# A gated linear attention and a two-layer block on one core: state sums moved from TensorE to VectorE, a new written-out order, and matmuls of a constant with itself

## The chip, the cores and the metric

The kernel runs on one core of one Trainium2 chip. A core has five engines that this kernel uses: TensorE (matrix products; its result goes to PSUM, eight banks), VectorE, ScalarE (activation functions), POOL (GpSimd) and SP (SyncE, which here only issues DMAs). The profile calls them PE, DVE, ACT, POOL and SP; PEld is TensorE's loading of weights. Each engine works through its own queue in the order in which the program was written, and waits at semaphores for the others. The metric is the time of one execution on the device in microseconds (us).

## The reference

Four inputs q, k, v and f_logit, each of shape (4, 8, 768, 48): batch, heads, steps, head dimension. For every head a state of 48 x 48 is carried over the steps, and its output goes through a two-layer block:

```python
f = 1.0 / (1.0 + np.exp(-f_logit))
for t in range(S):
    state = f[:, :, t, :, None] * state + np.einsum('bhd,bhe->bhde', k[:, :, t], v[:, :, t])
    y[:, :, t] = np.einsum('bhd,bhde->bhe', q[:, :, t], state)
x = y.transpose(0, 2, 1, 3).reshape(B * S, H * D)      # 3072 x 384
h = x @ w_in                                            # 384 x 2048
g = 0.5 * (h + np.sqrt(h * h + 4.0))
out = g @ w_out                                         # 2048 x 384
```

## The kernel before

**Blocks.** The 3072 rows are worked on in 12 blocks p of 256 steps; three blocks make one batch entry, so the state starts anew at p = 0, 3, 6 and 9. A block is held as two chunks (cc = 0 and 1) of 64 pairs of steps, for all 8 heads. Block 0 is loaded and prepared in two halves of four heads (`FINE`), named x = 0 and 1.

**Preparing a block.** `lf`, `lq`, `lk`, `lv` load 384 KB each (SP's queue). `ex` takes exp(-f), `ut` adds 1 (VectorE), `tt` multiplies the two steps of a pair, `ln` takes the logarithm (ScalarE). `hi` rounds it to float16 and `lo` keeps the rest, so that `cu` (TensorE, lines 234 and 239) can form cumulative sums over the chunk from two float16 terms. Block 0 (`DIRECT`) takes float32 terms instead, without `hi` and `lo`. `ep` and `ea` are exponentials of these sums, `ge`, `gs`, `gb` the small decay factors of a chunk. `qu`, `ku`, `qm`, `km` multiply q and k by these (POOL or VectorE, all at the helper's line 138; `qm` and `km` are two instructions each), `vc` casts v.

**Attention of a block.** For blocks 0 to 3 `tp` transposes q and k on TensorE and `te` copies them out of PSUM; from block 4 on a transposing DMA (`tx`) does it. `sc` forms the scores, `pm` masks them (VectorE), `yt` multiplies them by v. `kv` forms what the chunk adds to the state. `yn` adds q times the incoming state `sn` to `yt`'s result, and `yc` copies y out. Blocks 0 to 3 transpose y on TensorE (`xp`, `xe`), the others by DMA (`xx`).

**The state.** The incoming state is added to `kv`'s sum in PSUM by a product with the identity, `ia` (TensorE, line 394). VectorE then multiplies the sum, from PSUM, by a factor: `sa` (line 401) gives the state for the second chunk, `sb` (line 408) that for the next block. `ia` is issued for every chunk but the first of a batch entry, 20 in all.

**The two layers.** For a block there are eight pieces `m1` (six products of 256 columns each, line 470) that put h into PSUM, `sq` and `rt` on ScalarE (square; square root over two pieces), `gt` on VectorE (line 495), and eight pieces `m2` (four products of 384 columns each, line 507) that add up the output of the two chunks; `ev` copies it out and `st` stores it. The weights are loaded by POOL's queue (`wi0` to `wi3`, `wo0` to `wo7`).

**The order.** The pieces above are only described in `describe`. The text `ORDER` names each in the order in which it is issued, with the engine that does it and the PSUM banks that it gets: `cu1.0:T@10` is the sum of block 1 on TensorE into banks 1 and 0. A piece that may run on several engines runs on the one named there. `TABLE:e` and `TABLE:s` load ScalarE's tables. The loop at line 608 goes through this text and issues the pieces; semaphores follow from the tiles that they read and write. The blocks overlap: while m1 and m2 of block p run, blocks p + 1 to p + 3 are prepared.

Of the kernel before, what the change touches and what calls it, by code (L numbers as in the profile page):

```python
# [18 lines left out]
DIRECT = [0]  # L19
# [3 lines left out]
NHL = 2  # L23
NQK = 3
DEPTH = {'f': 3, 'q': 3, 'k': 3, 'v': 3, 'UT': 3, 's': 2, 'ep': 2, 'ea': 2, 'v16': 4, 'ge': 3, 'gs': 4, 'gb': 3, 'qkT0': 2, 'qkT1': 2, 'pm00': 2, 'pm01': 2, 'pm10': 2, 'pm11': 2, 'sn0': 2, 'sn1': 2, 'y16': 2, 'xT': 5, 'hsq': 3, 'r16': 3, 'g': 4, 'os': 2}
# [6 lines left out]
ln2.0:A vc0.1:A lq2.0:S hi2.0:P pm0.00:D ep1.0:A gs0:P lo2.0:P ge1:A pm0.10:D vc0.0:A pm0.01:D ea1.0:A kv0:T@32 km1.0:P  # L32
ex3.0:A cu2.0:T@41 pm0.11:D lk2.0:S sa0:D yt0:T@60 ge2:A gs1:D yn0.1:T yc0.0:A qu1.0:D gb2:P lv1.0:S ep2.0:A qm1.0:D wi1:P
yc0.1:A ea2.0:A xp0.1:T@5 wi2:P xp0.0:T@7 ut3.0:D tp1.0:T@36 ex4.0:A lf5.0:S xe0.0:D tt3.0:P xe0.1:D te1.0.0:A te1.1.0:D
m1.0.0:T@4 wo3:P ln3.0:A ut4.0:D m1.0.1:T@0 wi3:P sq0.0:A qu2.0:D sc1.1:T@17 sq0.1:A hi3.0:P pm1.11:D TABLE:s rt0.0:A lo3.0:P
m1.0.2:T@5 pm1.10:D ia0.1:T lv2.0:S gb1:D cu3.0:T@3 tt4.0:D ku2.0:P sc1.0:T@67 sb0:D m1.0.3:T@1 pm1.00:D sq0.2:A pm1.01:D
sq0.3:A m1.0.4:T@2 km2.0:P rt0.1:A gt0.1:D m1.0.5:T@6 gt0.0:D sq0.5:A lk3.0:S gt0.3:D sq0.4:A vc1.0:P c13.0:D rt0.2:A gt0.2:D
qm2.0:P kv1:T@70 TABLE:e ep3.0:A gt0.5:D ia1.0:T yt1:T@41 sa1:D yn1.0:T lk4.0:S m1.0.6:T@5 gt0.4:D wo0:P ex5.0:A yn1.1:T
yc1.0:D ia1.1:T tp2.0:T@67 wo1:P lk5.0:S ea3.0:A ut5.0:D m1.0.7:T@2 vc2.0:P ln4.0:A te2.0.0:D xp1.0:T@4 ge3:A sq0.7:A sb1:D
tt5.0:P kv2:T@36 yc1.1:A te2.1.0:D sq0.6:A xp1.1:T@0 gs3:P ia2.0:T xe1.0:D gs2:P sc2.0:T@17 ln5.0:A wo2:P xe1.1:D sa2:D  # L40
TABLE:s rt0.3:A sc2.1:T@40 lq3.0:S wo4:P pm2.00:D ia2.1:T m1.1.0:T@3 ku3.0:P pm2.11:D m1.1.3:T@6 pm2.10:D m1.1.1:T@1 sq1.0:A
pm2.01:D m1.1.5:T@0 hi4.0:P sq1.1:A lv3.0:S gt0.7:D lo4.0:P yt2:T@47 rt1.0:A gt0.6:D yn2.1:T m1.1.2:T@2 hi5.0:P sq1.3:A
gt1.1:D wo5:P m2.0.00:T@5 lf6.0:S sq1.2:A yc2.1:D m2.0.10:T@1 ku5.0:P rt1.1:A gt1.0:D m1.1.7:T@7 sq1.5:A gt1.3:D m1.1.6:T@3
# [24 lines left out]
ln10.0:A m2.4.13:T ku9.0:P pm6.01:D ln11.0:A kv7:T@46 sq5.1:A ev4.1:D yt6:T@70 TABLE:s rt5.0:A ia7.0:T yc6.0:D yn6.1:T gs7:P
# [54 lines left out]
def describe(nc, W, ctx_tiles, aps):  # L123
# [4 lines left out]
    def eng(e):  # L128
        return getattr(nc, ENGINES[e])
# [23 lines left out]
    for p in range(NP):  # L153
# [9 lines left out]
        for x, (h0, h1) in enumerate(parts):  # L163
# [483 lines left out]
```

## Time and profile before

| | |
|---|---|
| time, median of 3 runs | 206.72 us (206.17 to 207.64) |
| the profiled execution: time | 205.34 us |
| the profiled execution: span from the first to the last instruction | 203.6 us |
| mean granted TensorE clock | 0.954 of full speed |
| DMA: moved | 32.87 MB, mean 161 GB/s over the span |
| costliest groups: m1 products (L470) | 576, 74.0 us |
| m2 products (L507) | 384, 71.6 us |
| VectorE `gt` (L495) | 96, 62.2 us |
| ScalarE `sq` (L479) and `rt` (L485) | 96 and 48, 54.7 and 50.6 us |
| POOL q and k products (L138, with ea and ep) | 40, 39.7 us |

The page of the profile gives the busy time of each engine, the span in 40 slices with a digit for the busy share, the chain of waits that ended last, and groups of instructions by line. A timeline row reads: start, duration, engine, line, operation, output and inputs, shape, count; in brackets the idle time before it and what ended that. A row of the chain reads: start, duration, engine, output, line, count. Matmuls are pipelined: their single durations overlap, so what one holds TensorE for is read from the distance of starts, as the chain does. A row of stretches gives the busy time and in brackets the number of instructions for each engine, then the granted clock, the DMA share and GB/s.

### The profile page before, as it was taken

How to read it: one execution, taken by the hardware profiler on the slowest of the kernel's cores; microseconds unless marked ns; L12 is line 12 of the kernel's file. 1: busy time of each engine (PE TensorE's matmuls, PEld its weight loads, DVE VectorE, ACT ScalarE, POOL GpSimd, SP SyncE). 2: the span in 40 equal slices, each digit the busy share in tenths (PEclk: the TensorE clock that was granted, in tenths of full speed). 3: DMA queues.
4: the chain of work that ended last, by engine and by line, in shares of the span. 5: the costliest groups of instructions: out<-in, count | busy, mean ns of one | idle time of the engine just before them, and what ended most of it. 6: DMA issues, size and time to landing. Idle time of an engine off the chain costs nothing.

```text
span 203.6 us, 5630 instructions
## 1 busy us (share of the span) xinstructions
PE 177.7 (87%) x2302; PEld 129.1 (63%) x2302; DVE 147.3 (72%) x285; ACT 154.9 (76%) x248; POOL 108.6 (53%) x135
## 2 busy tenths in 40 slices
PE   0556898799899999979999979789998999999990
PEld 0544575587657766757667857467775778677660
DVE  7649579999688997957978958818984778434650
ACT  4266679999958999769988987758886698968700
POOL 4226789899969979929679738695000000000001
PEclk9995579999999999999999999969999999999998
DMA  6999999999959799994899999932894100505305
GB/s 158 269 262 244 275 198 217 234 256 273 183 156 234 108 254 203 222 278 99 129 214 207 249 129 240 195 51 36 149 140 119 39 5 0 42 0 155 77 22 136
DMA packets 80537, 32.87 MB, mean 161 GB/s; under 512 B 73888, under 2 KB 80496, under 8 KB 80512
## 3 DMA queue, kind: packets, MB, share of 16 engines
q1 hardware_dynamic: 76688, 29.27, 69.1%
q0 software_dynamic: 3824, 3.24, 9.9%
q8 instruction: 18, 0.29, 0.6%
q14 instruction: 7, 0.06, 0.1%
HBM read 25.17 MB, written 4.72 MB: 147 GB/s over the span
## 4 chain that ended last, share of the span: by engine, by line
issue 32%; PE 26%; POOL 18%; DMA 15%; ACT 3%; DVE 2%; SPq 2%; POOLq 0%
PE ps L507 10%; POOL qk L138 6%; PE ps L470 6%; DMA q<-in_q_dram 4%; PE ps L234 4%; POOL k L138 4%; DMA xT<-y 3%; DMA wout<-in_moe_w_out_dram 3%; DMA v<-in_v_dram 2%; POOL wout L149 2%; DMA f<-in_f_logit_dram 2%; POOL v L135 2%; POOL hl L214 2%; PE ps L364 1%; PE ps L383 1%
## 5 line engine op out<-in xcount | busy, mean ns | idle before, releaser
L470 PE MATMUL ps<-xT,win 128*128 128x256 f16 x576 | 74.0, 277 | 5.1 <-DMA xT<-y 3.5
L495 DVE SCALAR_TENSOR_TENSOR g<-ps,r 128x512 f16<-128x512 f32 x96 | 62.2, 682 | 17.5 <-ACT r L485 17.3
L507 PE MATMUL ps<-wout,g 128*128 128x384 f16 x384 | 71.6, 326 | 2.4 <-DMA wout<-in_moe_w_out_dram 1.3
L479 ACT ACTIVATE hsq<-ps 128x512 f16<-128x512 f32 x96 | 54.7, 593 | 18.0 <-PE ps L470 17.3
L470 PEld LDWEIGHTS <-win 128*128 128x128 f16 x576 | 55.5, 99 | 17.2 <-DMA xT<-y 4.2
L485 ACT ACTIVATE r<-hsq 128x1024 f16<-128x1024 f16 x48 | 50.6, 1056 | 1.1
L507 PEld LDWEIGHTS <-g 128*128 128x128 f16 x384 | 36.2, 98 | 22.6 <-issue 1.7
L371 DVE TENSOR_TENSOR pm<-ps,mask 128x512 f16<-128x512 f32 x48 | 30.8, 682 | 5.2 <-PE ps L364 5.0
L527 POOL DMA_DIRECT2D out_dram<-os x1 | 0.6, 602 | 59.7 <-ACT os L133 59.7
L138 POOL TENSOR_TENSOR qk<-q,ea 128x384 f16<-128x384 f32 x20 | 19.9, 1014 | 4.7 <-DVE q L138 4.7
L138 POOL TENSOR_TENSOR qk<-k,ep 128x384 f16<-128x384 f32 x20 | 19.8, 1013 | 0.3 <-ACT ge L302 0.2
L138 POOL TENSOR_TENSOR k<-k,UT 128x768 f32<-128x768 f32 x10 | 18.1, 1815 | 1.7 <-DMA k<-in_k_dram 1.6
L178 ACT ACTIVATE f<-f 128x768 f32<-128x768 f32 (+1 forms) x13 | 10.3, 795 | 3.3 <-DMA f<-in_f_logit_dram 3.2
L138 POOL TENSOR_TENSOR UT<-UT 128x384 f32<-128x384 f32 (+1 forms) x8 | 7.8, 984 | 8.9 <-DVE UT L185 8.9
L214 POOL TENSOR_TENSOR hl<-s,hl 128x384 f16<-128x384 f32 x11 | 10.0, 912 | 4.8 <-ACT hl L133 4.7
L133 ACT COPY os<-ps 128x384 f32<-128x384 f32 x12 | 5.8, 480 | 8.6 <-PE ps L507 7.2
L401 DVE TENSOR_TENSOR sn<-ps,gs 128x384 f16<-128x384 f32 x12 | 6.6, 554 | 7.7 <-PE ps L383 5.3
L135 POOL CAST v<-v 128x768 f16<-128x768 f32 x10 | 8.2, 821 | 5.2 <-DMA v<-in_v_dram 5.2
L364 PE MATMUL ps<-qkT 48*64 48x128 f16 x384 | 9.4, 228 | 0.7 <-ACT qkT L133 0.6
L135 DVE COPY os<-ps 128x384 f32<-128x384 f32 x12 | 6.5, 552 | 4.8 <-PE ps L507 3.1
L262 ACT ACTIVATE ep<-ps 128x384 f32<-128x384 f32 (+1 forms) x13 | 6.0, 470 | 5.2 <-PE ps L239 5.0
L364 PEld LDWEIGHTS <-qkT 48*64 48x64 f16 x384 | 6.4, 110 | 4.9 <-issue 3.5
(74 smaller groups left out, 200.8 us busy)
## 6 DMA issues: line engine op xcount, KB each, us to landing
f<-in_f_logit_dram SPq DMA_DIRECT2D x11, 384.0 KB, 6.2
k<-in_k_dram SPq DMA_DIRECT2D x11, 384.0 KB, 5.4
q<-in_q_dram SPq DMA_DIRECT2D x11, 384.0 KB, 6.2
v<-in_v_dram SPq DMA_DIRECT2D x11, 384.0 KB, 5.2
out_dram<-os SPq DMA_DIRECT2D x22, 192.0 KB, 3.5
win<-in_moe_w_in_dram POOLq DMA_DIRECT2D x4, 384.0 KB, 7.5
wout<-in_moe_w_out_dram POOLq DMA_DIRECT2D x8, 192.0 KB, 6.5
f<-in_f_logit_dram SPq DMA_DIRECT2D x2, 192.0 KB, 2.9
```

Of the source, the lines that this page charges most:

```text
L135: eng(e).tensor_copy(out=o, in_=i)
L138: eng(e).tensor_tensor(out=o, in0=a, in1=b, op=ALU.mult)
L178: nc.scalar.activation(out=t, in_=t, func=AF.Exp, scale=-1.0)
L214: eng(e).tensor_tensor(out=hl[:, 1, hs, 0:D], in0=T["s", p][:, hs], in1=hl[:, 0, hs, 0:D], op=ALU.subtract)
L234: nc.tensor.matmul(out=o, lhsT=tri[:, m], rhs=t[:, hs, 0:D], start=(r == 0), stop=(r == len(terms) - 1))
L364: nc.tensor.matmul(out=T["sc", p, i, h][64 * cc:64 * cc + 64, j, :], lhsT=t[r, 1, j, i, :], rhs=t[r, 0, j], start=True, stop=True)
L371: nc.vector.tensor_tensor(out=T["pm", p, i, h], in0=T["sc", p, i, h], in1=K["mask"][:, i].unsqueeze(1).broadcast_to([128, 4, 128]), op=ALU ...
L470: nc.tensor.matmul(out=T["h", p, m][:, a], lhsT=K["win"][m // 2][:, j, m % 2 * 256 + a * 128:m % 2 * 256 + a * 128 + 128], rhs=T["xT", p][ ...
L479: nc.scalar.activation(out=T["hsq", p, r][:, a], in_=T["h", p, m].rearrange("p a c t -> p (a c t)"), func=AF.Square, scale=1.0)
L485: nc.scalar.activation(out=T["r16", p, r], in_=T["hsq", p, r], func=AF.Sqrt, scale=0.25, bias=1.0)
L495: nc.vector.scalar_tensor_tensor(out=T["g", p][:, 2 * m:2 * m + 2, :].rearrange("p a t -> p (a t)"), in0=T["h", p, m].rearrange("p a c t - ...
L507: nc.tensor.matmul(out=T["o", p, cc], lhsT=T["g", p][:, jn, cc * 128:(cc + 1) * 128], rhs=K["wout"][jn // 2][:, jn % 2, :], start=(jn == 0 ...
```

## The change

Four things change.

- **State sums.** For blocks 3 to 11 (`SADD`) `ia` is no longer issued: 15 fewer products, 5 are left. A new piece `sp` on VectorE adds the incoming state to `kv`'s sum, from PSUM into an SBUF tile `st`; it is issued 12 times, where the sum is needed further on. `sa` or `sb` then multiplies `st` by the factor, on POOL in all 12 cases. The first chunk of a batch entry needs no sum; there, and in blocks 0 to 2, `sa` and `sb` stay on VectorE and read PSUM.
- **Block 0** is no longer in `DIRECT`: its cumulative sums come from float16 terms as in the other blocks. `hi` is written by ScalarE as a second logarithm, straight into float16 (`HI_ACT`); `lo` is added. The float32 copies of the constants are no longer made, and the triangles come from four VectorE instructions instead of eight (`tri2` is laid out with its two parts exchanged).
- **A new order.** `ORDER` is written anew: another order on every queue, SP's and POOL's too, other banks, and another engine for 75 of the pieces that both orders have, `sa` and `sb` among them. Net of all moves VectorE gives up 5 `gb` and `gs`, 3 `tt`, 3 `qu`, 1 `qm` and gets 3 `ku`, 5 `lo` (one of them a new one of block 0), 1 `km`; the weight loads are issued as wi0, wi2, wi1, wi3 and wo4, wo0, wo1, wo2, wo5, wo3, wo6, wo7. In block 0 `ex1` stands behind the four logarithms. Of the last block's four stores the two of the first chunk go to POOL's queue and the two of the second to SP's; before, one of the second went to POOL's and the others to SP's.
- **Constant matmuls.** A word `wmN:T@b` in the order issues N products of the float16 identity (128 x 128) with itself into bank b; nothing reads them. There are five such words: 27 ahead of block 0's transposes, 4 ahead of `cu1`, 26 ahead of `kv0` (bank 3), 4 ahead of `xp0.0`, 5 ahead of the first `m1`. That makes 66.

Pieces for lists that are empty here (`SPLIT`, `PMACT`) are left out of the diff below.

```diff
-DIRECT = [0]
+DIRECT = []
+SADD = [3, 4, 5, 6, 7, 8, 9, 10, 11]
+HI_ACT = [0]
...
-lf0.1:S lf0.0:S lf1.0:S lk0.0:S lk0.1:S TABLE:e ex0.1:A lq0.1:S ut0.1:D ex0.0:A tt0.1:D lq0.0:S ut0.0:D lf2.0:S tt0.0:P
-ex1.0:A lv0.1:S ku0.0:D ln0.0:A lv0.0:S ln0.1:A cu0.0:T@01 ut1.0:D cu0.1:T@01 ku0.1:D ep0.0:A qu0.1:P lk1.0:S ea0.0:A tt1.0:D
-ea0.1:A qu0.0:D ge0:A ep0.1:A qm0.0:D lf3.0:S ln1.0:A km0.0:D ex2.0:A km0.1:D tp0.0:T@23 hi1.0:A lq1.0:S qm0.1:D te0.1.0:A
-lo1.0:P tp0.1:T@23 te0.0.0:A te0.1.1:D lf4.0:S wi0:P te0.0.1:A ut2.0:D sc0.0:T@45 tt2.0:D sc0.1:T@67 cu1.0:T@10 ku1.0:D
...
+lf0.0:S lf0.1:S lk0.1:S lf1.0:S lk0.0:S TABLE:e ex0.0:A lq0.0:S ut0.0:D ex0.1:A tt0.0:P lq0.1:S ut0.1:D hi0.0:A lv0.0:S
+tt0.1:D ln0.0:A hi0.1:A lo0.0:D lf2.0:S ln0.1:A ku0.1:D cu0.0:T@01 ex1.0:A lo0.1:P ku0.0:D cu0.1:T@01 ep0.0:A lk1.0:S km0.0:D
+qu0.0:P ut1.0:D ea0.1:A lq1.0:S ep0.1:A tt1.0:D qu0.1:D ln1.0:A qm0.1:D lv0.1:S ea0.0:A km0.1:D ex2.0:A qm0.0:D wm27:T@2
+tp0.1:T@23 hi1.0:A lf3.0:S ut2.0:D tp0.0:T@23 ge0:A te0.1.1:A lo1.0:D tt2.0:P te0.1.0:A te0.0.1:D wm4:T@4 cu1.0:T@45 lf4.0:S
+te0.0.0:A ku1.0:D lk2.0:S wi0:P ln2.0:A sc0.1:T@67 sc0.0:T@10 ge1:A vc0.0:A gs0:P pm0.10:D qu1.0:P hi2.0:A lq2.0:S pm0.01:D
+vc0.1:A wi2:P lo2.0:D ea1.0:A wm26:T@3 kv0:T@32 pm0.11:D ex3.0:A cu2.0:T@60 qm1.0:P pm0.00:D ep1.0:A ea2.0:A sa0:D lv1.0:S
+yt0:T@57 km1.0:D yn0.1:T gb1:P yc0.0:A yc0.1:A wm4:T@4 xp0.0:T@4 ut3.0:D wi1:P ep2.0:A xp0.1:T@1 tp1.0:T@03 ge2:A xe0.1:D
+ex4.0:A tt3.0:P xe0.0:D te1.0.0:D wm5:T@5 m1.0.1:T@5 gs2:P ln3.0:A ut4.0:D m1.0.0:T@7 sq0.1:A hi3.0:P te1.1.0:D ia0.1:T
+m1.0.4:T@6 sq0.0:A lf5.0:S gs1:P gb2:P sb0:D TABLE:s rt0.0:A sc1.0:T@14 ku2.0:P sc1.1:T@03 pm1.01:D m1.0.5:T@2 pm1.10:D wi3:P
+km2.0:D sq0.5:A m1.0.2:T@4 tt4.0:P lq3.0:S sq0.4:A gt0.0:D m1.0.3:T@0 rt0.2:A pm1.11:D lo3.0:P lv2.0:S pm1.00:D sq0.2:A
+vc1.0:P cu3.0:T@7 gt0.4:D sq0.3:A rt0.1:A qu2.0:P gt0.5:D kv1:T@31 ia1.0:T c13.0:D yt1:T@62 qm2.0:P TABLE:e ep3.0:A sa1:D
+yn1.0:T gt0.3:D ia1.1:T yn1.1:T lk3.0:S m1.0.6:T@3 yc1.0:D ex5.0:A wo4:P gt0.2:D tp2.0:T@06 ge3:A wo0:P lq4.0:S ut5.0:D
...
+m2.10.13:T m2.11.03:T ev10.1:D m2.10.03:T ev11.0:D m2.11.11:T st11.0.1:P ev10.0:A m2.11.12:T st10.01.1:S st11.0.0:P
+st10.01.0:S m2.11.13:T ev11.1:A st11.1.1:S st11.1.0:S
...
+                    direct = p in HI_ACT
+
+                    def hi(e, bk, x=x, hs=hs, p=p, direct=direct):
+                        o = K["hl"][p % NHL][:, 0, hs, 0:D]
+                        if direct:
+                            nc.scalar.activation(out=o, in_=T["UT", p][:, 1, hs], func=AF.Ln)
+                        else:
+                            copy(e, o, T["s", p][:, hs])
...
-                                         stop=(i == 1 and j == 3 and first and cc == 0), skip_group_check=True)
+                                         stop=(i == 1 and j == 3 and (p in SADD or (first and cc == 0))), skip_group_check=True)
...
+            added = p in SADD
+            if not (cc == 0 and first) and not added:
                 def ia(e, bk, cc=cc, p=p):
...
+            if added and not (cc == 0 and first):
+                def sp(e, bk, cc=cc, p=p):
+                    T["st", p, cc] = sb(f"st{cc}", p, [128, 4, 2, 48], FP32)
+                    nc.vector.tensor_tensor(out=T["st", p, cc], in0=T["u", p, cc], in1=T["sn", p, cc], op=ALU.add)
...
+                def sm(e, bk, cc=cc, p=p, nxt=nxt, factor=factor):
+                    T["sn", nxt[0], nxt[1]] = sb(f"sn{1 - cc}", nxt[0], [128, 4, 2, 48], FP16)
+                    mul(e, T["sn", nxt[0], nxt[1]], T["st", p, cc], factor())
...
-        for x in range(2):
-            nc.vector.tensor_scalar(out=tri[l, x, m], in0=tri2[l, 1 - x], scalar1=1.0, scalar2=None, op0=ALU.subtract)
-            nc.vector.tensor_copy(out=tri[g, x, m], in_=tri2[g, 1 - x])
...
+        nc.vector.tensor_scalar(out=tri[l, :, m], in0=tri2[l], scalar1=1.0, scalar2=None, op0=ALU.subtract)
+        nc.vector.tensor_copy(out=tri[g, :, m], in_=tri2[g])
...
+            if name.startswith("wm"):
+                t = ps(banks, [128, 128], FP32)
+                for n in range(int(name[2:])):
+                    nc.tensor.matmul(out=t, lhsT=ident, rhs=ident, start=True, stop=True)
+                continue
             W.pieces[name].emit(e or W.pieces[name].eng, banks)
```

More of the change, by code (lines that the diff above doesn't have):

```diff
@@ L389, in describe @@
         for cc in range(2):
-            if cc == 0 and first:
-                pass
-            else:
+            added = p in SADD
+            if not (cc == 0 and first) and not added:
                 def ia(e, bk, cc=cc, p=p):
@@ L603, in ps @@
         return psp.tile(shape, dt, name=f"ps{bank}", tag=f"ps{bank}", bufs=1)
-    K = {"s32": s32, "tri32": tri32, "ind32": ind32, "hl": hl, "qk": qk, "tri": tri, "ind": ind, "half": half, "ident": ident, "mask": mask, "win": win, "wout": wout}
+    K = {"s32": s32, "l32": l32, "tri32": tri32, "ind32": ind32, "hl": hl, "qk": qk, "tri": tri, "ind": ind, "half": half, "ident": ident, "mask": mask, "win": win, "wout": wout}
     W = Work()
```

436 lines of the change are left out of this document (242 added, 194 removed).

## The prediction

> **What bounds the kernel now.** I read the page first (busy shares and slices), then the stretches by ten microseconds, then the chain of waits, and last the timeline of the places where TensorE stands still. The profiled execution took 205.34 us, 203.6 of them its span; the median of the three runs shown is 206.72, so 1.38 is added to whatever the sum gives for the profiled execution.
>
> ```profile
> PE 177.7 (87%) x2302; PEld 129.1 (63%) x2302; DVE 147.3 (72%) x285; ACT 154.9 (76%) x248; POOL 108.6 (53%) x135
> ...
> PEclk9995579999999999999999999969999999999998
> ```
> ```profile
> 0.00:10.00 10.00, 2.54 (x8) 2.55 (x9) 6.78 (x33) 3.67 (x6) 3.71 (x14) 1.00 0.94 213
> 10.00:20.00 10.00, 6.19 (x90) 4.29 (x90) 6.84 (x16) 6.21 (x17) 4.03 (x6) 0.72 1.27 253
> 20.00:30.00 10.00, 8.89 (x138) 6.40 (x136) 6.41 (x14) 6.95 (x13) 7.99 (x11) 0.60 1.13 241
> 30.00:40.00 10.00, 7.96 (x165) 5.98 (x163) 9.63 (x18) 9.74 (x16) 9.02 (x10) 1.00 1.15 220
> 40.00:50.00 10.00, 9.83 (x148) 7.68 (x142) 9.15 (x18) 9.79 (x15) 9.88 (x14) 1.00 1.24 262
> 50.00:60.00 10.00, 8.69 (x117) 5.85 (x115) 7.71 (x16) 7.69 (x14) 7.82 (x8) 1.00 0.78 164
> ...
> 57.70:199.00 141.30, 135.88 (x1687) 97.70 (x1684) 102.63 (x178) 110.90 (x172) 66.85 (x77) 0.99 0.68 136
> ```
>
> Columns: stretch, length, then busy time of PE, PEld, DVE, ACT and POOL (instructions in brackets), granted clock, DMA share, GB/s. Three stages can be seen. Up to 30 us nothing is full but the DMA engines: the first block goes from engine to engine, and TensorE runs half its time at a reduced clock. From 30 to 50 VectorE, ScalarE and POOL are all above 90%. From 57.7 to the last matmul TensorE is busy 135.88 of 141.30 us: there it is the bound, and what leaves TensorE's queue there leaves the time. It stands still for 5.42 us in that stage, nearly all of it in four places:
>
> ```profile
> 88.04 0.83 PE L470 MATMUL ps<-xT,win 128*128 128x256 f16 x6 [1.47 <-DMA xT<-y]
> ...
> 120.97 0.82 PE L507 MATMUL ps<-wout,g 128*128 128x384 f16 x4 [1.13 <-DVE g L495]
> ...
> 133.21 0.93 PE L470 MATMUL ps<-xT,win 128*128 128x256 f16 x6 [2.00 <-DMA xT<-y]
> ...
> 157.53 0.52 PE L383 MATMUL ps<-v,qk 64*128 64x96 f16 x16 [0.76 <-ACT os L133]
> ```
>
> **The change part by part.**
>
> *State sums.* For blocks 3 to 11 the 15 products `ia` with the identity go. In the chain such a product holds TensorE between these two lengths:
>
> ```profile
> 77.62 0.27 PE ps L394
> ...
> 101.21 0.16 PE ps L394
> ```
> ```profile
> L401 DVE TENSOR_TENSOR sn<-ps,gs 128x384 f16<-128x384 f32 x12 | 6.6, 554 | 7.7 <-PE ps L383 5.3 <-PE ps L394 2.3
> ...
> L408 DVE TENSOR_TENSOR sn<-ps,gb 128x384 f16<-128x384 f32 x8 | 4.4, 550 | 0.5 <-PE ps L394 0.5
> ...
> L138 POOL TENSOR_TENSOR q<-q,UT 128x384 f32<-128x384 f32 x6 | 6.0, 997 | 0.0
> ```
>
> 15 x 0.16 to 15 x 0.27 is 2.4 to 4.0; the middle, 15 x 0.21 = 3.15, is my value. All 15 lie after 57 us, in the stage that TensorE bounds. VectorE keeps its number of state instructions: 20 multiplications before; after, 8 multiplications and 12 new sums `sp`, of the same size and one PSUM input, so 12 x 0.55 = 6.6 us goes and 6.6 comes. The 12 other multiplications go to POOL. The trace has none there on a state tile; the nearest row, a POOL product of 128x384, is 0.997 us, so POOL gains 12.0 us. After 57.7 it is busy 66.85 of 141.30, so these cost nothing while the waits between the engines have slack (the slower rival is where they have none). `sa` and `sb` read `sp`; `yn` of the second half waits for `sa`, and behind `yn` on TensorE's queue stand the m1 and m2 products.
>
> *Block 0.* Its cumulative sums were float32 products; now they are float16 products of a high and a low part:
>
> ```profile
> 7.46 2.93 PE ps L234 x8
> 10.38 1.12 PE ps L239 x8
> ...
> 69.59 0.33 PE ps L234 x2
> 69.91 0.18 PE ps L239 x8
> ```
> ```profile
> 8.61 0.93 POOL L138 TENSOR_TENSOR q<-q,UT 128x192 f32<-128x192 f32 x1 [2.08 <-DMA q<-in_q_dram]
> ...
> 12.11 0.36 DVE L138 TENSOR_TENSOR qk<-q,ea 128x192 f16<-128x192 f32 x1 [2.35 <-ACT ea L262]
> ```
>
> The float32 products took 2.93 + 1.12 = 4.05 us. The float16 ones are eight of half the width of the row at 69.59 (8 x 0.083 = 0.66) and sixteen of the narrow kind (16 x 0.0225 = 0.36): 1.02. The path gets 3.0 shorter on TensorE and longer by `lo`, a product of 128x192 like the 0.36 row, and a second logarithm about as long: 0.7. ScalarE's `ex1` is also moved behind these logarithms, and VectorE's constants lose their float32 copies. But the q products cannot go ahead of q's load: the first of them ran at 12.11 and could run no earlier than 8.61 + 0.93 = 9.54. Bounds of the gain 0 to 2.6; I take 2.0, near the upper end, since the sum of the parts (3.0 - 0.7) is 2.3.
>
> *The constant matmuls.* The order holds 27 + 4 + 26 + 4 + 5 = 66 of them, one more than the title says.
>
> ```profile
> 14.30:28.00 13.70, 10.71 (x172) 7.49 (x171) 9.95 (x20) 8.73 (x19) 10.01 (x14) 0.50 1.19 252
> ...
> 134.00:135.00 1.00, 1.00 (x6) 0.65 (x5) 0.00 (x0) 0.82 (x2) 1.00 (x2) 0.50 0.05 8
> ```
> ```profile
> L340 PEld LDWEIGHTS <-qk x4: 92/94/95, 12.5 to 12.5; 64*128 64x128 f16 x4
> ```
> ```profile
> L340 PEld LDWEIGHTS <-qk x14: 102/126/128, 14.7 to 15.0; 64*128 64x128 f16 x14
> ```
> ```profile
> 24.38 0.82 PE L454 MATMUL ps<-ident,y 128*128 128x128 f16 x6 [0.90 <-ACT y L133]
> ```
> ```profile
> 69.42 0.17 PE ps L454 x3
> ```
>
> From 14.3 to 28.0 the granted clock is 0.50, and TensorE's 10.71 busy us would be 5.4 at full clock. Not all of the difference is on the path: in the same stretch VectorE has 9.95 us of work and POOL 10.01, so the stretch of 13.7 cannot get shorter than about 10. Bounds 0 to 3.7; I take the middle, 2.0. What the 66 cost: a product of this shape takes 0.17 / 3 = 57 ns at full clock and at most 0.82 / 6 = 137 ns at half, so 3.8 to 9.0 us in all, in time when TensorE waits (3.8 of its 10 us from 10 to 20). 27 stand ahead of block 0's transposes, which wait for VectorE. The 26 are the ones to watch: they write bank 3, so they wait for the copies of the transposes out of it, and `kv0` and all of TensorE's queue stand behind them for 1.5 us (26 x 57 ns), or 3.6 if the clock is at half. `kv0` waits for ScalarE's two `vc0` anyway; at full clock I cost them at nothing.
>
> [...]
>
> *The new order.* [...] I take 1.0 gained, with bounds from 5 gained to 5 lost. From 30 to 50 us the three full engines have the same work as before, with the DMA engines at 220 to 262 GB/s: of the 4.0 gained at the start I count 1.0 given back there, for loads that then have to come earlier.
>
> *The end.* Both last stores go to SP's queue, where before POOL took one:
>
> ```profile
> 198.80 1.25 SPq L527 DMA_DIRECT2D out_dram<-os  x2
> 198.97 0.48 ACT L133 COPY os<-ps 128x384 f32<-128x384 f32 x1 [5.77 <-PE ps L507]
> 199.74 0.60 POOL L527 DMA_DIRECT2D out_dram<-os  x1 [59.66 <-ACT os L133]
> ```
>
> SP's last issue ended at 200.05; a second one of 1.25 / 2 = 0.6 ends at 200.65, POOL's ended at 200.34: 0.3 lost.
>
> *Sum.* 3.15 + (2.0 + 2.0 - 1.0) + 1.0 - 0.3 = 6.85 us. The span becomes 196.75, the profiled execution 198.5, the median 206.72 - 6.85 = 199.9.
>
> **The rivals.** (1) *Only the 15 products count.* The start is hidden by the loads and by the full stage, and the clock falls anyway in another window: 206.7 - 3.15 + 0.3 = 203.9, give or take 1.5. For it: DMA share above 1.1 from 10 to 50. Against: TensorE is the longest wait there, not a load. (2) *All of it comes.* Start 2.6 + 3.7, products 3.15, gaps 3: 206.7 - 12.45 + 0.3, about 194.5; with part of it, 196 to 198. (3) *Slower: the state path on POOL.* POOL takes its queue in order, and a pair of its q or k products is 2 x 0.997 = 2.0 us. Where such a pair stands ahead of `sa`, `yn` waits up to 2.0, and TensorE with it; the trace shows half clock after the one gap of 2.00 us, another 1.7. Each such place costs 3.7; two of the twelve take away the whole gain, and three give 199.9 + 11.1 = 211.0. Against: after 57.7 POOL is idle half the time. (4) *The constant matmuls hold up block 0.* The clock drops before them, so 2.0 is not gained and the 26 take up to 3.6 on the path, half of it beside the wait for `vc0`: 199.9 + 2.0 + 1.8 = 203.7. (5) *Slower: VectorE and POOL hold each other up.*
>
> ```profile
> 30.10 0.92 DVE L138 TENSOR_TENSOR gb<-gs,ge 128x8 f32<-128x8 f32 x1
> ```
> ```profile
> 29.19 1.81 POOL L138 TENSOR_TENSOR k<-k,UT 128x768 f32<-128x768 f32 x1
> ```
>
> This product of 8 elements took 0.92 us and ended at 31.02, when POOL's ended at 31.00. If each of the 12 new POOL products held VectorE up for as long, and all of it were on the path, 12 x 0.92 = 11 us would make 210.9. [...]
>
> **How the numbers follow.** Chances: forecast (198 to 202.5) 0.42; rival 2 (under 198) 0.15; rivals 1 and 4 together 0.30, of which 0.20 is below 204.65; rival 3 0.09; rival 5 0.04, of which, with 3, 0.02 comes out level. A measurement of this kernel tells about 1%, 2.07 us, from no change: faster means under 204.65, slower over 208.79. Faster 0.42 + 0.15 + 0.20 = 0.77, same 0.10 + 0.02 = 0.12, slower 0.11. The range from 196.0 to 206.5 leaves out some 0.06 of rival 2 and 0.14 of the slow cases. The likeliest time is 199.9.
>
> **What would show it.** Right: 5 products of `ia` instead of 20; first m1 product two or more us before 26.1; granted clock at 1.00 for most of 14 to 28; TensorE idle under 5 us after its stream becomes continuous. Wrong: TensorE waiting on `yn` for POOL's `sn`; `kv0` directly behind 26 products at 0.50; VectorE's small products growing from their size to POOL's. New gaps of over 2 us in the long stage, with half clock behind them, would make the prediction wrong by 3.7 each.

## The result and the profile after

The changed kernel takes 198.88 us (median of 4 runs, 197.65 to 206.46) against 206.44 (205.95 to 207.64): a ratio of 0.9605, with a 95% interval of 0.9524 to 0.9687. The forecast was 199.9, with a range of 196.0 to 206.5. In run 1 below the same kernel came out at 0.9669 (0.9608 to 0.9731). The ratios here and below leave out executions that were disturbed and the medians do not, so where the two differ the ratio counts; 0.01 of it is 2.07 us. The profiled execution took 197.65 us, 195.4 of them its span, where before it was 205.34 and 203.6.

The page of the changed kernel (busy times, and the granted clock in 40 slices):

```profile
PE 175.8 (90%) x2353; PEld 128.5 (66%) x2353; DVE 152.6 (78%) x278; ACT 156.0 (80%) x250; POOL 117.7 (60%) x150
...
PEclk9999999999999999999999999999999999999999
```

Two of its stretches (same columns as before; the second runs from the first m2 product to the last):

```profile
30.00:40.00 10.00, 7.59 (x163) 5.34 (x162) 10.00 (x19) 8.71 (x16) 8.92 (x12) 1.00 1.09 226
46.37:191.00 144.63, 141.09 (x1774) 102.06 (x1773) 114.15 (x192) 120.05 (x186) 84.41 (x98) 1.00 0.77 148
```

The picture is the one of before, tightened: the full VectorE from 30 to 40, then TensorE as the bound, idle for 144.63 - 141.09 = 3.54 us in the long stage. Its gaps there, from the timeline of TensorE:

```profile
99.46 0.64 PE L416 MATMUL ps<-qkT 48*64 48x128 f16 x32 [1.22 <-DMA qkT<-qk]
...
110.17 1.48 PE L543 MATMUL ps<-xT,win 128*128 128x256 f16 x12 [0.56 <-DMA xT<-y]
...
145.41 0.64 PE L416 MATMUL ps<-qkT 48*64 48x128 f16 x32 [1.32 <-DMA qkT<-qk]
```

No gap is as long as the 2.00 us of before, and none has half clock behind it: the mean granted clock of the execution is 1.00. The groups that the state sums touch:

```profile
L454 PE MATMUL ps<-sn,ident 128*128 128x384 f16 x5 | 1.6, 330 | 0.1
...
L143 POOL TENSOR_TENSOR sn<-st,gb 128x384 f16<-128x384 f32 x6 | 5.0, 829 | 0.7 <-DVE gs L143 0.7
...
L143 POOL TENSOR_TENSOR sn<-st,gs 128x384 f16<-128x384 f32 x6 | 5.0, 829 | 12.9 <-DVE st L470 10.7 <-PE ps L503 2.0
```

Five `ia` are left. POOL's new products took 0.829 us each, and POOL itself waited 10.7 us for `st`. The waits of TensorE name no `sn` made by POOL.

How far the two layers have come by a given time shows where the time went. A stretch from 0 counts the m1 products (first row) and the m2 products (second row) done; here up to 140 us, before and after:

```profile
0.00:140.00 140.00, 47.52 (x364) 35.09 (x365) 0.94 0.98 201
0.00:140.00 140.00, 40.07 (x208) 19.16 (x208) 0.94 0.98 201
```
```profile
0.00:140.00 140.00, 50.83 (x402) 37.90 (x402) 1.00 1.03 204
0.00:140.00 140.00, 42.20 (x224) 20.86 (x225) 1.00 1.03 204
```

At full pace an m1 product holds TensorE 0.109 us (twelve from 23.55 to 24.86 in the changed kernel, shown below), and an m2 product, of 384 columns instead of 256, is taken at 1.5 times that, 0.1635, an estimate that the trace bears out (eight of them hold it from 49.01 to 50.31, 0.1625 each). Counts times these prices, in us of work done, for the kernels of which it is used here:

| by | before | old order, state sums only | old order, all parts | changed | changed, no constants |
|---|---|---|---|---|---|
| 60 us | 18.3 | 16.8 | 20.4 | 20.6 | 20.9 |
| 120 us | 63.4 | 61.3 | 64.7 | 64.3 | 65.4 |
| 140 us | 73.7 | 72.7 | 75.0 | 80.4 | 81.8 |
| 190 us | 116.9 | 115.9 | 118.9 | 124.8 | all done |

The changed kernel is 2.3 us ahead at 60, still 0.9 at 120, then 6.7 at 140 and 7.9 at 190. Most of the gain appears in the twenty microseconds in which the kernel before waited 2.00 us for `xT` and then ran at a granted clock of 0.50, from 134 to 137 us throughout. The table counts only m1 and m2, and the new order puts the other products of a block at other places, so a lead at one moment is a rough figure.

### The profile page after: what moved, and what is told of

The parts are those of the page before. It is cut to its first block, busy times and chain, and to the rows that moved or that the text cites. A ratio compares the mean times of both kernels' runs of the same rounds, so it can differ in the third digit from the quotient of the medians.

```text
span 195.4 us, 5725 instructions
## 1 busy us (share of the span) xinstructions
PE 175.8 (90%) x2353; PEld 128.5 (66%) x2353; DVE 152.6 (78%) x278; ACT 156.0 (80%) x250; POOL 117.7 (60%) x150
## 3 DMA queue, kind: packets, MB, share of 16 engines
q0 software_dynamic: 3872, 3.34, 10.7%
## 4 chain that ended last, share of the span: by engine, by line
PE 50%; DMA 18%; DVE 11%; POOL 9%; issue 5%; ACT 4%; SPq 1%; DVEq 0%; POOLq 0%
PE ps L580 23%; PE ps L543 19%; DMA win<-in_moe_w_in_dram 4%; DMA q<-in_q_dram 3%; DMA qkT<-qk 3%; DMA k<-in_k_dram 3%; POOL qk L143 3%; DMA v<-in_v_dram 2%; DMA xT<-y 2%; DVE pm L431 2%; PE ps L416 2%; DVE qk L143 2%; DVE g L568 2%; PE ps L494 2%; POOL q L143 1%
## 5 line engine op out<-in xcount | busy, mean ns | idle before, releaser
L543 PEld LDWEIGHTS <-win 128*128 128x128 f16 x576 | 54.6, 98 | 14.2 <-DMA win<-in_moe_w_in_dram 2.2
L143 POOL TENSOR_TENSOR qk<-q,ea 128x384 f16<-128x384 f32 x22 | 22.5, 1042 | 0.3 <-ACT ea L314 0.2
L143 POOL TENSOR_TENSOR qk<-k,ep 128x384 f16<-128x384 f32 x18 | 17.6, 1001 | 0.2
L143 POOL TENSOR_TENSOR UT<-UT 128x384 f32<-128x384 f32 (+1 forms) x11 | 11.3, 1030 | 8.1 <-DVE UT L233 7.5
L285 PE MATMUL ps<-hl,tri 128*128 128x384 f16 (+1 forms) x34 | 8.5, 355 | 6.5 <-DVE UT L233 5.4
L143 POOL TENSOR_TENSOR sn<-st,gs 128x384 f16<-128x384 f32 x6 | 5.0, 829 | 12.9 <-DVE st L470 10.7
L143 POOL TENSOR_TENSOR k<-k,UT 128x768 f32<-128x768 f32 x7 | 12.7, 1815 | 0.0
L143 POOL TENSOR_TENSOR q<-q,UT 128x384 f32<-128x384 f32 (+1 forms) x10 | 10.1, 1008 | 3.4 <-DMA q<-in_q_dram 3.4
L233 DVE TENSOR_SCALAR UT<-f 128x768 f32<-128x768 f32 (+1 forms) x13 | 9.4, 737 | 1.2 <-ACT f L183 1.1
L140 DVE COPY os<-ps 128x384 f32<-128x384 f32 x14 | 7.6, 550 | 3.2 <-PE ps L580 1.7
```

What stands on the lines that cost most here:

```text
L140: eng(e).tensor_copy(out=o, in_=i)
L143: eng(e).tensor_tensor(out=o, in0=a, in1=b, op=ALU.mult)
L233: eng(e).tensor_scalar(out=T["UT", p][:, 0::2, hs], in0=T["f", p][:, hs].rearrange("p h i d -> p i h d"), scalar1=1.0, scalar2=None, op0=A ...
L285: nc.tensor.matmul(out=T["cum", p, m][:, h0 * D:h1 * D], lhsT=tri[:, m], rhs=t[:, hs, 0:D], start=(r == 0), stop=(r == len(terms) - 1), sk ...
L543: nc.tensor.matmul(out=T["h", p, m][:, a], lhsT=K["win"][m // 2][:, j, m % 2 * 256 + a * 128:m % 2 * 256 + a * 128 + 128], rhs=T["xT", p][ ...
```

## The experiments

**1. The changed kernel again**, on the chip of runs 2, 3 and 4.

> The changed kernel itself once more, beside the others. Theory (15 products less, a shorter start, fewer gaps) and rivals alike: 198 to 200 us. What is looked for is the start: in the first profile the 27 constant matmuls took 3.04 us (113 ns each), half pace, although the clock row reads 1.00. If the array always starts at half pace here, they take about 3.0 again; if its state at the start differs from execution to execution, they may take 1.5.

Measured: 202.22 us median (199.35 to 206.36), ratio 0.9669 (0.9608 to 0.9731), which is 199.9 on the scale of the 206.7 before. In its trace the 27 products take 3.04 us again: the half pace at the start came back.

**2. The new order without the constant products.**

```diff
-wm27:T@2 ... wm4:T@4 ... wm26:T@3 ... wm4:T@4 ... wm5:T@5
```

> The changed kernel without its 66 constant matmuls, nothing else changed. Theory (the clock is worth some 2 us at the start): half pace lasts to about 28 us instead of 18, and 2 to 3 us are lost: 200.5 to 202. Rival A (the constant matmuls are most of the gain): 204 or more. Rival B (they are worth nothing, the start is bound by loads and the other engines): 198 to 199.5.

> The new order and the state sums without the 66 constant products, a second time on another chip. Theory (the constant products gain nothing; the clock that they raise early is given back right behind them): a ratio to the kernel before of 0.950 to 0.962 again, so a time of 196 to 198.5. Rival (the first measurement was a favourable chip): 0.962 to 0.970, as the changed kernel itself.

Measured: 196.76 (196.0 to 199.12), 0.9533 (0.9480 to 0.9586); on another chip 197.66 (195.5 to 199.57), 0.9529 (0.9468 to 0.9589). Without the 66 products the kernel is faster, by 0.0136 x 206.7 = 2.8 us against run 1 on the same chip, whose interval lies wholly above; against the first ratio on record, 0.9605, it is 1.5, and there the intervals overlap. Why the products gain nothing is in the two timelines of TensorE. First the changed kernel:

```profile
14.28 1.46 PE L285 MATMUL ps<-hl,tri 128*128 128x384 f16 x4
...
16.86 2.38 PE L698 MATMUL ps<-ident 128*128 128x128 f16 x26
19.29 0.51 PE L444 MATMUL ps<-v,qk 64*128 64x96 f16 x16
19.74 0.82 PE L285 MATMUL ps<-hl,tri 128*128 128x384 f16 x4
...
23.55 1.47 PE L543 MATMUL ps<-xT,win 128*128 128x256 f16 x12
24.86 0.33 PE L454 MATMUL ps<-sn,ident 128*128 128x384 f16 x1
25.75 0.83 PE L543 MATMUL ps<-xT,win 128*128 128x256 f16 x6 [0.56 <-DMA win<-in_moe_w_in_dram]
```

And the same kernel without them:

```profile
16.98 0.67 PE L445 MATMUL ps<-v,qk 64*128 64x96 f16 x12 [0.38 <-ACT v L139]
17.58 1.46 PE L286 MATMUL ps<-hl,tri 128*128 128x384 f16 x4
...
22.47 2.62 PE L544 MATMUL ps<-xT,win 128*128 128x256 f16 x12
24.93 0.33 PE L455 MATMUL ps<-sn,ident 128*128 128x384 f16 x1
25.86 0.83 PE L544 MATMUL ps<-xT,win 128*128 128x256 f16 x6 [0.60 <-DMA win<-in_moe_w_in_dram]
```

The products do raise TensorE's pace: `cu2`, four sums of the same form, takes 0.82 us with them and 1.46 without, and the first twelve m1 products 1.47 instead of 2.62. But the 26 hold `kv0` up: it starts at 19.29, where without them its last twelve products start at 16.98. So the first m1 product comes 1.1 us later. By 24.9 both kernels stand level, and both then wait for the same weight load. What the constants cost comes after that: at 140 us the changed kernel is 1.4 us behind, and its gaps shown above (1.22 and 1.32 us for `qkT`, 0.56 for `xT`) stand against these and one of 0.30 in the kernel without:

```profile
94.63 0.83 PE L544 MATMUL ps<-xT,win 128*128 128x256 f16 x6 [0.65 <-DMA xT<-y]
...
147.62 1.47 PE L544 MATMUL ps<-xT,win 128*128 128x256 f16 x12 [0.81 <-DVE os L141]
```

**3. The constant products alone**, put into the order of before at the same places.

```diff
-... km0.1:D tp0.0:T@23 ... sc0.0:T@45 ... kv0:T@32 ... xp0.1:T@5 ... m1.0.0:T@4
+... km0.1:D wm27:T@2 tp0.0:T@23 ... wm4:T@4 sc0.0:T@45 ... wm26:T@3 kv0:T@32 ... wm4:T@5 xp0.1:T@5 ... wm5:T@4 m1.0.0:T@4
```

> The kernel before with 66 constant matmuls put into its order (27 ahead of block 0's transposes, 4 ahead of its scores, 26 ahead of kv0, 4 ahead of xp0, 5 ahead of the first m1) and nothing else. Theory: full pace from 14 us on, 2 us gained: 204 to 205. Rival A: 4 us or more gained, 202.5 or less. Rival B: no change, 206 to 207.

Measured: 208.76 (203.54 to 211.44), 0.9945 (0.9883 to 1.0007). The interval reaches from 204.3 to 206.9 us. Rival A is out; the theory's 204 to 205 and rival B's 206 to 207 both reach into it, so this run does not tell a gain of 2.0 us from none.

**4. All parts in the order of before**: state sums, block 0 in float16, constants.

```diff
-DIRECT = [0]
+DIRECT = []
+SADD = [3, 4, 5, 6, 7, 8, 9, 10, 11]
+HI_ACT = [0]
...
-ia3.1:T ... sb3:D
+sp3.1:D ... sb3:P
```

> The old order with all other parts of the change: state sums on VectorE with the multiplications on POOL, block 0 in float16 terms with the four logarithms ahead of ex1, the constant matmuls as in old_const. Theory (3.15 for the products, some 3 at the start, the rest from the order): 199.5 to 201.5. Rival C (the order is most of it): 203 or more. Rival D (the order gives nothing): 198 to 199.5.

Measured: 207.0 (203.73 to 209.04), 0.9968 (0.9916 to 1.0020). That is rival C: nearly all of the gain needs the new order. The profiled execution (203.73) is 2.1 us ahead at 60 and 2.0 at 190: of the 15 products nothing arrives. The timeline of TensorE shows what is late in their stead:

```profile
131.73 2.74 PE L544 MATMUL ps<-xT,win 128*128 128x256 f16 x12 [3.55 <-DMA xT<-y]
```

This is the wait of 133.21 in the kernel before, grown from 2.00 to 3.55, with half clock behind it again (twelve m1 products in 2.74, and a mean granted clock of 0.83 from 130 to 140 us). SP's timeline in this kernel reads:

```profile
122.68 2.71 SPq L376 DMA_TRANSPOSE qkT<-qk  x1
125.44 0.63 SPq L601 DMA_DIRECT2D out_dram<-os  x1
126.16 1.33 SPq L519 DMA_TRANSPOSE xT<-y  x1
```

The y that it transposes was copied out by 123.8; its transpose stands 2.4 us behind that, after another one of 2.71 us and a store, and lands 131.73 - 126.16 = 5.6 us after its issue began. In the kernel before y was ready at 127.0, its transpose stood behind the same two for 2.3 us, and the distance from issue to landing was 133.21 - 129.23 = 4.0:

```profile
125.36 3.10 SPq L323 DMA_TRANSPOSE qkT<-qk  x1
128.51 0.63 SPq L527 DMA_DIRECT2D out_dram<-os  x1
129.23 1.31 SPq L445 DMA_TRANSPOSE xT<-y  x1
```

So the stand in SP's queue is the same in both and did not make the wait grow. TensorE came 3.0 us earlier (128.2 against 131.2) and y was ready 3.2 us earlier, but the transposed y only 1.5, since its landing took 1.6 us longer. Why it did is not shown.

**5. The state sums alone** in the order of before.

```diff
+SADD = [3, 4, 5, 6, 7, 8, 9, 10, 11]
...
-ia3.1:T ... sb3:D
+sp3.1:D ... sb3:P
```

> The order before, with the state sums on VectorE and the 12 state products on POOL as the only edit. By the sum of the prediction 15 x 0.21 = 3.15 us go: 203.5. Theory as it stands after the run with all parts in the old order (the waits for xT at 88 and 133 us are set by VectorE, ScalarE and the DMA, and swallow what leaves TensorE ahead of them): 205 to 207, a ratio of 0.99 to 1.00. Rival (the constants or block 0 cost there what the sums gained): 202.5 to 204.5.

Measured: 207.52 (204.76 to 212.68), 1.0010 (0.9962 to 1.0058). My sum asked for 203.5. In the table its profiled execution (206.57) is 1.5 us behind the kernel before at 60, when none of the 15 `ia` would have run yet, and still 1.0 behind at 190: of 3.15 us 0.5 came through. The expectation was met, at its edge, in its number, but only in a small part by its mechanism. At 88 us TensorE does not wait at all, since it comes later: both kernels are level at 88.70. Then it waits at places where the kernel before does not, and is 2.5 us behind at 115:

```profile
96.97 0.82 PE L543 MATMUL ps<-xT,win 128*128 128x256 f16 x6 [0.63 <-DVE os L140]
...
104.78 0.48 PE L416 MATMUL ps<-qkT 48*64 48x128 f16 x16 [0.48 <-ACT ep L314]
...
107.33 0.81 PE L543 MATMUL ps<-xT,win 128*128 128x256 f16 x6 [0.66 <-DVE pm L431]
...
134.69 1.67 PE L543 MATMUL ps<-xT,win 128*128 128x256 f16 x7 [2.42 <-DMA xT<-y]
```

With one more of 0.26 at 114.61, the new waits for VectorE and ScalarE are 2.03 us; the wait for `xT` grew only from 2.00 to 2.42. What makes VectorE and ScalarE late there is not shown: the run takes the products out and puts the state on its new path over POOL in one edit, and no run parts the two in the old order.

**6. The 15 products put back into the new order** (on TensorE, 384 columns, into banks that the next m1 overwrites; nothing reads them), without the constants.

```diff
+if name == "xi":
+    nc.tensor.matmul(out=ps(banks, [128, 384], FP32), lhsT=ident, rhs=win[0][:, 0, 0:384], start=True, stop=True)
+    continue
```

> The changed kernel without constant matmuls, with the 15 products of 384 columns back on TensorE (constant times weights, result unused), each ahead of the first m1 product behind the kv of its block; the state sums stay on VectorE. Theory (after the start TensorE is the bound, so what stands in its queue is paid in full at 0.16 to 0.27 us each): 2.4 to 4.0 us slower than new_no_const, 199 to 201. Rival (the gain came from the order, and TensorE's queue has slack for 15 products): 0 to 1 us, 196.5 to 197.8.

Measured: 199.64 (198.9 to 203.04), 0.9683 (0.9622 to 0.9744). Against run 2 that is 2.9 us by the medians and (0.9683 - 0.9533) x 206.7 = 3.1 by the ratios. So 15 products of this size cost 3 us in the new order, where taking 15 out of the old one, together with the new path of the state, gained nothing. And with the 15 in place the new order and block 0 are still 0.0317 x 206.7 = 6.6 us faster than the kernel before.

**7. Constants where TensorE has nothing to do**: 28 ahead of block 0's first sums, 27 behind them, none ahead of `kv0`, and without the three words of 4, 4 and 5.

```diff
-... wm27:T@2 tp0.1:T@23 ... wm26:T@3 kv0:T@32 ...
+... wm28:T@0 cu0.0:T@01 ... cu0.1:T@01 ... wm27:T@2 ... tp0.1:T@23 ... kv0:T@32 ...
```

> The changed kernel with constant matmuls only where TensorE waits anyway: 28 ahead of its first product (cu0) and 27 behind cu0, none ahead of kv0. Full pace should come at 8 to 11 us instead of 18 (changed kernel) or 23.6 (without constants). Theory (the third m1 product waits for its weights at 25.8 us with or without constants, so pace at the start is worth nothing): 196 to 197.5. Rival (the clock is worth its 2 us once nothing is held up): 194 to 195.5.

Measured: 198.65 (197.63 to 202.98), 0.9644 (0.9570 to 0.9719). Both expectations missed: no constant holds anything up here, and by the ratios it is 2.3 us slower than no constants in run 2 all the same (on another chip, and with intervals that just overlap). Its clock row on the page, and from its timeline the constants behind the sums and the first m1 products:

```profile
PEclk9995899999999999999999999999999999999998
```
```profile
7.64 1.67 PE L699 MATMUL ps<-ident 128*128 128x128 f16 x27
...
22.88 1.49 PE L544 MATMUL ps<-xT,win 128*128 128x256 f16 x12 [0.91 <-DMA win<-in_moe_w_in_dram]
...
25.58 0.83 PE L544 MATMUL ps<-xT,win 128*128 128x256 f16 x6 [1.05 <-DMA win<-in_moe_w_in_dram]
...
28.96 1.48 PE L544 MATMUL ps<-xT,win 128*128 128x256 f16 x12 [1.22 <-DMA win<-in_moe_w_in_dram]
```

Here the 27 constant products take 62 ns each, where the first 27 of the changed kernel took 113; TensorE is at full pace by 7.6 us. A granted clock of half follows in the fourth slice (14.8 to 19.7 us; 0.50 from 15 to 20, 0.92 from 20 to 25), and then TensorE waits for each weight load in turn. The loads are the bound at this point, so a faster TensorE only waits longer: the products at 28.96 start at 28.93 in the changed kernel and at 28.51 without constants.

**8. Block 2's two k products moved to POOL**, once with the constants and once without.

```diff
-km2.0:D
+km2.0:P
```

> The changed kernel, constants kept, with one edit: block 2's two k products (km2) on POOL instead of VectorE. Theory (lock: these two VectorE products wait until POOL's queue has a gap, 2.2 us in one execution and 4.6 in the other, and TensorE then stands still and falls to half clock): the upper part of the spread goes, all executions within 196.5 to 200, median 198. Rival (the spread comes from the clock or from the constants themselves): 199 to 206 as in after_again.

> The new order without the constant products, and block 2's two k products (the pair that took VectorE between 1.2 and 4.6 us) moved to POOL, which then holds 2.0 us more ahead of block 1's v copy. Theory (the pair costs only where POOL has no gap, and without the constants POOL has one): no gain at the median, 0.950 to 0.962, but no execution above 199.5. Rival (VectorE is late in this stage in any case, and 1.2 us less of it counts): 0.940 to 0.948.

Measured: 199.3 (198.41 to 202.42), 0.9677 (0.9609 to 0.9744) with the constants; 196.94 (196.15 to 198.8), 0.9541 (0.9483 to 0.9599) without. With the constants the theory missed: two of its six executions took more than 200 us. Without them it came out as expected, no gain and none above 199.5. TensorE waits for POOL where it had waited for VectorE (timeline of the kernel with constants):

```profile
31.64 0.32 PE L286 MATMUL ps<-hl,tri 128*128 128x384 f16 x1 [1.50 <-POOL hl L269]
```

**9. Whether VectorE and POOL hold each other up.** In the new order this pair of k products takes very different times (the pair on VectorE and POOL's product beside it, first in the changed kernel, then in the one without constants):

```profile
28.61 0.92 POOL L268 TENSOR_TENSOR hl<-s,hl 128x384 f16<-128x384 f32 x1
```
```profile
28.18 2.24 DVE L143 TENSOR_TENSOR qk<-k,ep 128x384 f16<-128x384 f32 x2
```
```profile
27.73 0.92 POOL L269 TENSOR_TENSOR hl<-s,hl 128x384 f16<-128x384 f32 x1
```
```profile
28.30 1.24 DVE L144 TENSOR_TENSOR qk<-k,ep 128x384 f16<-128x384 f32 x2
```

To see whether POOL makes the difference, POOL gets products that nothing reads ahead of block 1's v copy: one, then two.

```diff
-vc1.0:P
+pf:P vc1.0:P
...
+if name == "pf":
+    nc.gpsimd.tensor_tensor(out=scr[:, 1], in0=scr[:, 0], in1=scr[:, 0], op=ALU.mult)
+    continue
```

> The changed kernel without constant matmuls, with one more POOL product of 128x384 (1.0 us, result unused) ahead of block 1's v cast, where POOL waited 0.6 us for the load; POOL then works without a gap from block 2's k product on. Lock theory: VectorE's two km2 products grow from 1.24 us to 3 to 5, TensorE waits 2 us more behind them, 198.5 to 201.5. Rival (no lock; POOL is only 0.4 us later): 196.5 to 197.5, the two products at 1.0 to 1.3.

> The new order without the constant products, with two float32 products of 128x384 that nothing reads put on POOL ahead of block 1's v copy, so that POOL has no gap while VectorE's pair of k products runs. Theory (a lock: VectorE's product of two SBUF tiles gets in only where POOL has a gap): the pair takes 2.5 to 5 us instead of 1.24, and TensorE waits for VectorE behind it; time 2 to 4 us over the kernel without the fill. Rival (no lock, both engines only share bandwidth): the pair takes 1.2 to 2 us, and the time rises by at most 1.

Measured: 197.79 (196.88 to 201.25), 0.9586 (0.9521 to 0.9651) with one; 197.71 (197.25 to 198.37), 0.9559 (0.9503 to 0.9614) with two. With one, POOL was idle for 0.79 us ahead of the copy all the same, and the pair ran in that gap: this run decides nothing.

```profile
29.09 1.01 DVE L144 TENSOR_TENSOR qk<-k,ep 128x384 f16<-128x384 f32 x2
```

With two there was no gap (POOL first, then VectorE):

```profile
27.53 0.92 POOL L269 TENSOR_TENSOR hl<-s,hl 128x384 f16<-128x384 f32 x1
28.40 2.31 POOL L704 TENSOR_TENSOR scr<-scr 128x384 f32<-128x384 f32 x2
30.67 0.81 POOL L141 CAST v<-v 128x768 f16<-128x768 f32 x1
```
```profile
27.64 2.38 DVE L144 TENSOR_TENSOR qk<-k,ep 128x384 f16<-128x384 f32 x2
```

That is just under the 2.5 that the theory asked for and above the rival's 2, but it does not show that the fill did it. In run 2's second execution, the same kernel without the fill on the same chip, the pair took as long, where POOL's gap ahead of the copy was short (POOL first, then VectorE):

```profile
28.82 0.86 POOL L141 CAST v<-v 128x768 f16<-128x768 f32 x1 [0.25 <-DMA v<-in_v_dram]
```
```profile
27.75 2.34 DVE L144 TENSOR_TENSOR qk<-k,ep 128x384 f16<-128x384 f32 x2
```

What does show that the pair waits for POOL is when it ends. In four traces (the changed kernel, run 2's first, runs 6 and 7) POOL's product ahead of the copy (`hl`) ends at 29.53, 28.65, 28.61 and 28.53 us, a gap follows, and the pair, begun 1.35, 0.35, 0.69 and 0.51 us before that end, is over 0.89, 0.89, 0.89 and 0.90 us after it. So the pair's 2.24, 1.24, 1.58 and 1.41 us read as a wait for POOL and some 0.9 us of work, and that wait is counted in the trace as busy time of VectorE. It goes the other way too: with the fill POOL's two products took 2.31 instead of 2 x 0.83 = 1.66 (one alone took 0.83 in the run before), 0.65 us longer. The time did not rise by 2 to 4: 0.9559 against 0.9529 on the same chip is 0.6 us, well inside the intervals. Each engine's wait for the other is there; no price of it on the path can be seen here.

## Why the prediction was right, and which of its steps were not

The time came out 1.0 us from the forecast. Of the 8.2 us that the span lost, the table and the runs give 2.3 to the start (the lead at 60 us), 3.1 to the 15 products (run 6), and 0.3 to the end (4.4 us from the last m2 product instead of 4.67); the rest, 2.5, is left for the order. My terms were 3.0, 3.15, -0.3 and 1.0. Of this division only the 3.1 was measured by an edit; the lead of 2.3 was down to 0.9 by 120 us.

- *State sums, 3.15.* Right in size in the new order, 2.9 to 3.1 against bounds of 2.4 to 4.0. The reason I gave was wrong: "All 15 lie after 57 us, in the stage that TensorE bounds". In the same stage of the old order nothing came of taking them out (run 5), since other waits of TensorE opened, most of them for VectorE and ScalarE. A share of 96% busy did not say that an instruction less is time less.
- *Block 0, 2.0, and the first m1 product "two or more us before 26.1".* It starts at 23.55, and at 22.47 without the constants, 3.6 earlier. The new order's start is part of that, and block 0 was not run by itself, so how the 3.6 divides stays open.
- *Constant matmuls, 2.0.* The failed step, and outside its bounds: not 0 to 3.7 gained but 1.5 to 2.8 lost (run 2); in the old order run 3 leaves it open, between 2.4 gained and 0.1 lost. Two steps were wrong. One is "at full clock I cost them at nothing": the 26 ahead of `kv0` ran mostly at half pace, 2.38 us, and `kv0` stood behind them. The other is that the half clock of 14.3 to 28.0 was priced as if its end would show; the weight loads behind it end at nearly the same time (run 7). Rival 4 had the place and the price (up to 3.6), and the higher pace gave it back by 24.9. The clocks of the kernel before hint at the same: of its executions that the ratios of the runs count, the 18 with a mean granted clock of 0.989 or more have a median of 206.05 us, the 10 at 0.968 or less 206.58. Each group scatters over more than 3.5 us, so the 0.5 between them is a rough figure, but it is not 2.0.
- *The weight loads of 92 to 95 ns at 12.5 us* in the kernel before, against a median of 126 at the granted 0.50, stand behind 4.05 us of float32 products (7.46 to 11.5); no run took these products out alone, so whether they made the loads fast is not shown. In the changed kernel, whose first sums are float16, the start is slow: the same four sums take 1.46 us at 14.28 and 0.82 at 19.74 in one execution. The granted clock in the profile's rows does not show this: it reads 1.00 throughout in the changed kernel.
- *The new order, 1.0 with bounds of 5.* No run shows the 1.0; 2.5 is left over. It is worth more than this, though, since without it the other parts come to nearly nothing (run 4: 0.3%). What the trace of before shows is the four gaps, 5.4 us, and the half clock behind the third of them:

```profile
133.00:134.00 1.00, 0.79 (x7) 0.68 (x8) 0.00 (x0) 0.00 (x0) 1.00 (x2) 0.90 0.98 137
134.00:135.00 1.00, 1.00 (x6) 0.65 (x5) 0.00 (x0) 0.82 (x2) 1.00 (x2) 0.50 0.05 8
135.00:136.00 1.00, 1.00 (x20) 0.53 (x20) 0.00 (x0) 0.37 (x2) 1.00 (x2) 0.50 0.00 0
136.00:137.00 1.00, 1.00 (x42) 0.92 (x34) 0.00 (x0) 0.97 (x2) 1.00 (x2) 0.50 0.00 0
137.00:138.00 1.00, 1.00 (x15) 0.87 (x12) 0.83 (x2) 0.47 (x1) 1.00 (x2) 0.89 0.06 16
```

  By these rows it lasted 0.2 + 3.0 + 0.2 = 3.4 us, and half of that, 1.7, is my estimate of what it cost. With the gaps that makes 7.1 us, of which I gave the order a seventh.
- *The end, -0.3.* There was no loss: +0.3.
- *Rival 3* did not occur: no wait of TensorE for POOL's `sn`, and the product takes 0.829, less than my 0.997. Its 3.7 for each such place is the gap of 2.00 and the 1.7 behind it, taken from that one place.
- *Rival 5* is real in that each waits for the other: in run 9 the pair is over 0.89 or 0.90 us after POOL's product in all four traces, and POOL's two products took 2.31 us beside the pair where 1.66 was due. My sign for it ("VectorE's small products growing") was there while the kernel was faster. As a price it failed: neither more of it (two products) nor less (run 8) moved the time beyond the intervals.

So the sum was right by luck: two errors cancelled. Without the constants the span is 193.8, 9.8 less than before; 3.1 of that are the 15 products, and 6.7 stand where I had 2.0 + 1.0 - 1.0 - 0.3 = 1.7 for block 0, the order, what is given back and the end: 5.0 too little. The constants then cost 195.4 - 193.8 = 1.6 in the same two executions, where I had 2.0 gained: 3.6 too much.

What stays open is why the constants cost 1.5 to 2.8 us after both kernels stood level. Part of it can be placed: near 100 us TensorE waits for `qkT`, 1.22 us in the changed kernel, 2.51 in run 7 and 1.53 in run 8 with constants, and not at all in both executions of run 2 (of the other traces without constants only run 8's has this wait, 1.23 us). Why `qkT` comes later is not shown. A stretch of half clock is not needed for it: the profiled execution of the changed kernel has a granted clock of 1.00 throughout and is still 1.6 us longer than that of run 2. It may add to it elsewhere: of the executions that the ratios count, those with constants (the result, runs 1 and 7) have mean granted clocks of 0.946 to 1.0 and those without (run 2) 0.988 to 1.0. No run changed the clock alone.

The best version found is the new order without the constants: 0.953 of the time before, twice.

## What to carry to other kernels

Price a removed instruction by the waits that follow it, even on an engine that is 96% busy: in one order taking 15 products out gave nothing, and other waits opened behind them, and in another order 15 of the same size cost 3 us. Products that only raised TensorE's pace gained nothing here, where a weight load ended last behind them (TensorE went on at 25.75 us with them and at 25.86 without), and they held up its queue (the first m1 product at 23.55 against 22.47): they cost 1.5 to 2.8 us. And a new order is best tested with the other edits left in and taken out, since what they are worth depends on it.

## What the runs showed of the hardware that I had not expected

- In the changed kernel and in run 2 TensorE's first products run at half pace although the granted clock reads 1.00 (in run 2 twelve m1 products take 2.62 us, where they take 1.47 later), and stay there long: without constants from 11.7 us on to 24.9, with small gaps (0.38 us at 16.98), with them until some time within the 26 products of 16.86 to 19.24, which take 92 ns each, between the 113 of the first 27 and the 62 of run 7.
- VectorE's products of two SBUF tiles grew, and so did `ut`, which adds 1 to one tile, although the change does not touch what they do; it does move them beside other work of POOL. For one pair of products run 9 shows POOL as the reason; for the groups it is not shown. Groups of VectorE, before and after:

```profile
L185 DVE TENSOR_SCALAR UT<-f 128x768 f32<-128x768 f32 x11 | 6.3, 590 | 0.4 <-POOL v L135 0.4
...
L138 DVE TENSOR_TENSOR qk<-k,ep 128x384 f16<-128x384 f32 x2 | 1.0, 548 | 0.0
```
```profile
L233 DVE TENSOR_SCALAR UT<-f 128x768 f32<-128x768 f32 x11 | 8.7, 805 | 0.1
...
L143 DVE TENSOR_TENSOR qk<-k,ep 128x384 f16<-128x384 f32 x4 | 3.3, 855 | 0.0
```

  11 x 0.215 + 4 x 0.307 = 3.6 us of VectorE's time in these two groups alone.
- One transposing DMA of `qkT` held SP's queue for 2.7 and 3.1 us (rows of run 4), one of `xT` for 1.3, and what stands behind waits even with its data ready: y at 123.8 in run 4, its transpose issued at 126.16.
